# An FNet mixing layer and a gated feed-forward block on one core: a fifth unit of the sequence DFT as seven block products, and a planner that orders the DFTs' work

## The chip, the cores and the metric

The kernel runs on one core of a Trainium2 chip. The metric is device time in microseconds from launch to end, the median of three runs. Lower is better. The names of the engines in the profile are PE (TensorE, matrix products; PEld is its weight load), DVE (VectorE), ACT (ScalarE), POOL (GpSimd) and SP (SyncE, which here issues all DMAs).

## The reference

Two sublayers, each with a layernorm before it and a residual sum behind it, on 2048 tokens of 448 features, all in float32:

```python
def _A_ref(x, dft_seq_re, dft_seq_im, dft_hid_re, dft_hid_im):
    a = jnp.einsum("bsd,ed->bse", x, dft_hid_re)
    b = jnp.einsum("bsd,ed->bse", x, dft_hid_im)
    y = jnp.einsum("ts,bse->bte", dft_seq_re, a) - jnp.einsum("ts,bse->bte", dft_seq_im, b)
    return y

def _B_ref(x, w_gate, w_up, w_down):
    g = jnp.einsum("bsd,df->bsf", x, w_gate)
    u = jnp.einsum("bsd,df->bsf", x, w_up)
    h = _gelu(g) * u
    return jnp.einsum("bsf,fd->bsd", h, w_down)

x = A_x
h = x + _A_ref(_layernorm(x, axis=-1), A_dft_seq_re, A_dft_seq_im, A_dft_hid_re, A_dft_hid_im)
h2 = h + _B_ref(_layernorm(h, axis=-1), B_w_gate, B_w_up, B_w_down)
```

The feed-forward width is 1792. The DFT matrices are inputs, so the kernel multiplies by them as by any matrix.

## The kernel before

**Numbers.** Each float32 operand is split in two float16 parts: ACT writes the high part (`hi_part`, a scaled copy, line 105), DVE writes the low part as source minus high part (`lo_part`, lines 109 and 111). A product then takes three matmuls: high by high, high by low, low by high. So every operand of PE costs ACT and DVE one pass each, and DVE waits for ACT in it.

**Feature DFT (F).** The 16 tiles of 128 tokens are normalized (`x_stats`, `x_root`, `x_rstd`, `x_norm`, `x_lo`), transposed by DMA (`x_turn`; the first four by PE), and multiplied with both hidden matrices by `feature_mm` (line 422), 22 matmuls of 448 columns each, into two PSUM banks `ab`. `feature_out` takes the banks out: into `b`.

**Sequence DFT (U).** It has 8 passes `p`, each for 256 output tokens, and in each pass 8 units `u` of 256 input tokens (two tiles, `cc`). Unit (p, u) needs a block `wr` of both sequence matrices, 128 x 1024 in float32, loaded by `seq_load`, split into `ws` by `seq_split`, and multiplied with the `b` of its two tiles by `seq_mm` (line 518). A *plain* unit does this with 24 matmuls of 448 columns. A *product* unit (`is_s(u)`) uses a scheme of seven products for a 2 by 2 block product: 42 matmuls of 224 columns. For that DVE makes four sums of the block first (`seq_sums`, lines 480 to 482, into `wsum`), the split has seven slots and not four, and on the `b` side GpSimd makes sums of the tile's four halves (`feature_sums`, lines 460 to 462, on `b32`), which `feature_split` then splits. Units 4 to 7 are product units, 0 to 3 plain. `seq_out` takes a pass out of PSUM into `h`, and ACT and DVE then prepare the layernorm of the block that follows (`ffn_moments`, `ffn_norm_act`, `ffn_sums`, `ffn_split`, `ffn_transpose`).

**Weights of the gate and up products.** There are 14 rows `f` of weights. Ten of them are summed and split during the DFTs (`Weights`, `gu_raw` to `gu_w`) and stored in DRAM as `w_dram[f]`, whole; the last three in the order (2, 0, 1) also stay in SBUF as the first weights used. Four (`LATE`: 4, 7, 10, 13) are prepared later. Nine of the ten rows' tiles `gu_w`, and the `b32` of the product tiles, take turns in one ring of two buffers, tag `w`.

**What sets the order.** Each engine does its instructions in the order in which the program issues them, and SP its DMAs too. In the DFTs PE's work is a list of 80 slots (16 F, 64 U). All other work is hung on slots by hand: `plan(n, rank, what)` puts work ahead of slot `n`, for instance

```python
for g, (p, u) in enumerate(units):
    n = where["U", p, u]
    if is_s(u):
        plan(n - 3, 6, lambda p=p, u=u: seq_sums(p, u))
    if g:
        plan(n - 2, 3, lambda p=p, u=u: seq_split(p, u))
```

**After the DFTs.** A loop over 56 tiles `t` (four quarters of the tokens by 14 rows; line 970) does the gate and up products of `GateUp`: its PSUM banks X, Y and Z are opened, copied (`pY`, `u`) and closed in turn, ACT does the copies and the gelu. In the first quarter (t = 0 to 13) the weights of the down product are prepared beside that by `down_prep`: GpSimd sums (`down_sums`, `wd_s`), ACT high parts (`down_hi`), DVE low parts. From t = 14 on the down product (line 913) runs too.

Of the kernel before, what the change touches and what calls it, by code (L numbers as in the profile page):

```python
# [32 lines left out]
def kernel(  # L33
# [262 lines left out]
    S_UNITS, WR = (4, 5, 6, 7), 3  # L296
    ORDER = (0, 1, 5, 2, 6, 3, 7, 4)
# [141 lines left out]
    def feature_out(i):  # L439
        ps = feat.pop(i)  # L440
        if not is_s(i // 2):
            t = bop[i] = dft.tile([P, 2, 4, HD], F16, name=f"b{i}")
            for r in range(2):
                src, sc = ps[r][:, :D], (SC_AB, -SC_AB)[r]
                hi_part(t[:, 0, 2 * r : 2 * r + 2].rearrange("p o d -> p (o d)"), src, sc)
                lo_part(
                    t[:, 1, 2 * r : 2 * r + 2].rearrange("p o d -> p (o d)"),
                    src,
                    t[:, 0, 2 * r : 2 * r + 2].rearrange("p o d -> p (o d)"),
                    sc,  # L450
                )
            return
        b = b32[i] = ring.tile([P, 8, HD], F32, tag="w", bufs=2, name=f"b32_{i}")
        for r in range(2):
            hi_part(b[:, 2 * r : 2 * r + 2].rearrange("p o d -> p (o d)"), ps[r][:, :D], (SC_AB, -SC_AB)[r])


# [6 lines left out]
    def feature_split(i):  # L464
        b = b32.pop(i)
        t = bop[i] = dft.tile([P, 2, 7, HD], F16, name=f"b{i}")
        hi_part(t[:, 0], b[:, 1:8])
        lo_part(t[:, 1], b[:, 1:8], t[:, 0])
# [4 lines left out]
    def seq_load(p, u):  # L473
        wr[p, u] = dft.tile([P, 4, 2 * P], F32, tag="wr", bufs=4, name=f"wr{p}_{u}")
        nc.sync.dma_start(wr[p, u], w_seq[p * N_UNIT + u])

    def seq_sums(p, u):
        r = wr[p, u]
        s = wsum[p, u] = dft.tile([P, 4, 2 * P], F32, tag="wsum", bufs=2, name=f"wsum{p}_{u}")
        V.tensor_add(s[:, 0:2], r[:, 1:2].to_broadcast([P, 2, 2 * P]), r[:, 0:4:3])  # L480
        V.tensor_add(s[:, 2], s[:, 1], r[:, 0])
        V.tensor_add(s[:, 3], s[:, 2], r[:, 2])  # L482

    def seq_split(p, u):
        r = wr.pop((p, u))
        t = ws[p, u] = dft.tile([P, 2, 7, 2 * P], F16, tag="ws", bufs=3, name=f"ws{p}_{u}")
        parts = [(slice(0, 1), r[:, 0:1]), (slice(1, 3), r[:, 2:4]), (slice(3, 7), wsum.pop((p, u)))] if is_s(u) else [(slice(0, 4), r)]
        for dst, src in parts:
            hi_part(t[:, 0, dst], src, D_SC)
        for dst, src in parts:  # L490
            lo_part(t[:, 1, dst], src, t[:, 0, dst], D_SC)

# [15 lines left out]
    def seq_mm(p, u, first, last):  # L508
# [4 lines left out]
        for cc in range(2):  # L513
# [7 lines left out]
            if is_s(u):  # L521
                for a, o, k, half in PRODUCTS:
                    for m, (lb, lw) in enumerate(TERMS):
                        mm(k, slice(half * HD, half * HD + HD), w[:, lw, a, cc * P : (cc + 1) * P], b[:, lb, o], end and m == 2)
            else:
                for k, a0 in ((0, 0), (1, 1)):
                    for r in range(2):
                        for m, (lb, lw) in enumerate(TERMS):
                            rhs = b[:, lb, 2 * r : 2 * r + 2].rearrange("p o d -> p (o d)")
                            mm(k, slice(0, D), w[:, lw, a0 + 2 * r, cc * P : (cc + 1) * P], rhs, end and r == 1 and m == 2)  # L530
# [112 lines left out]
    for n, s in zip((2, 4, 6, 7), S_UNITS):  # L643
        mixed.insert(n, s)
# [12 lines left out]

    for k, (i, i2) in enumerate(tiles_of):
        n = where["F", i]
        if k >= 2:  # L660
            if k > 2:
                plan(n - 10, 8, lambda u=i // 2: x_load(u))
            if k > 2:
                plan(n - 7, 7, lambda i=i, j=i2: x_stats(i, j))
                plan(n - 6, 2, lambda i=i, j=i2: x_root(i, j))
                plan(n - 6, 5, lambda i=i, j=i2: x_rstd(i, j), lambda i=i, j=i2: x_bias(i, j))
            for c in (i, i2):
                n = where["F", c]
                if k > 2:
                    plan(n - 5, 5, lambda i=c: x_norm(i), lambda i=c: x_lo(i))  # L670
                plan(n - 4, 2, lambda i=c: x_turn(i))
        for c in (i, i2):
            n = where["F", c]
            if k:
                plan(n + 1, 1, lambda i=c: feature_out(i))
            if is_s(c // 2):
                plan(n + 1, 6, lambda i=c: feature_sums(i, G))
                plan(n + 2, 4, lambda i=c: feature_split(i))
    for g, (p, u) in enumerate(units):
        n = where["U", p, u]  # L680
        if is_s(u):
            plan(n - 3, 6, lambda p=p, u=u: seq_sums(p, u))
        if g:
            plan(n - 2, 3, lambda p=p, u=u: seq_split(p, u))
        if g < 4:
            if g:
                plan((-5, 1, 2)[g - 1], 9, lambda p=p, u=u: seq_load(p, u))
        else:
            plan(where["U", *units[g - 4]] - 2, 9, lambda p=p, u=u: seq_load(p, u))
# [3 lines left out]

    pairs = [where["F", 2 * u] for u in ORDER if is_s(u)]
    early_f = [s + 4 for s in pairs[1:3]]
    n0 = p1_end + 15
# [3 lines left out]
    order = list(reversed(in_dft[2:])) + in_dft[:2]  # L700

    def gu_begin(f):
        gu[f] = Weights(f, p2, lambda: w_tile(f"gu_w{f}", ring if f != 2 else ring3))

    late_f = N_DFT - len(early_f)
    at_f = early_f + [n0 + k * (len(slots) - 5 - n0) // late_f for k in range(late_f)]
    plan(0, 9, lambda: gu_begin(order[0]))
    for k, f in enumerate(order):
        n = at_f[k]
        plan(n, 7, lambda f=f: gu[f].sums())  # L710
        plan(n + 1, 7, lambda f=f: gu[f].split(True))
        if k + 1 < N_DFT:
            plan(n + 2, 9, lambda f=order[k + 1]: gu_begin(f))
        plan(n + 2, 7, lambda f=f: gu[f].split(False))
        plan(n + 3, 10, lambda f=f: gu[f].store())

    for p in range(N_PASS):
        q, j = divmod(p, 2)
        n = max(where["U", p, u] for u in range(N_UNIT)) + 1
        if p < 2:  # L720
            plan(n - 6, 9, lambda p=p: h_tile(p))
        else:
            n0 = min(where["U", p, u] for u in range(N_UNIT))
            plan(n0 - 5, 9, lambda p=p: h_tile(p))
            plan(n0 - 2, 4, lambda p=p: seq_seed(p))
        if p == N_PASS - 1:
            continue
        plan(n, 1, lambda p=p: seq_out(p))
        for g in range(2):
# [657 lines left out]
```

## Time and profile before

| | |
|---|---|
| median of 3 runs | 729.01 us (728.94 to 729.23) |
| the profiled execution | 729.15 us, of which the profile's span is 727.4 us |
| granted TensorE clock | 0.999 |
| busy share of the span | PE 97%, DVE 73%, ACT 54%, POOL 30% |
| DMA | 139.24 MB, 60.8% of 16 engines' span |
| first U slot to the end of the DFTs | 28.7 to 361.6 us |
| first quarter of gate and up | 361.6 to some 440 us |

How to read the lines that follow: a group's line has the source line, the engine, the operation, written and read tile with buffer numbers left out, the shape, the count, then busy time and mean ns of one, then the engine's idle time just before these instructions and what ended it. A timeline's line begins with start and length in us and ends with the idle time before it in brackets. A line of waits has who waited, for whom, the total, the number of times and the longest. Busy time of overlapping instructions of one engine is counted once.

### The profile page before, as it was taken

To read this page: it belongs to the slowest core of one execution; us is meant where nothing else is said; L and a number is where in the kernel's file an instruction comes from. 1 tells how busy PE (TensorE), PEld (TensorE's weight loads), DVE (VectorE), ACT (ScalarE), POOL (GpSimd) and SP (SyncE) were. 2 spreads that over 40 slices of the span, in tenths; PEclk is the share of its full clock that TensorE was granted. 3 is DMA by queue.
4 is the path that set the end of the run, shared out by engine and by line. 5 is a ranking of instruction groups with operands and counts; after the bars stand their busy time and mean duration, and the time that the engine had idled before them with its cause. 6 is when DMAs were issued, how large, how long until landed. Compare 5 with 4: busy or idle time off the path is not lost.

```text
span 727.4 us, 14930 instructions
## 1 busy us (share of the span) xinstructions
PE 708.2 (97%) x5944; PEld 574.1 (79%) x5944; DVE 529.1 (73%) x1054; ACT 396.1 (54%) x836; POOL 215.3 (30%) x241
## 2 busy tenths in 40 slices
PE   7999997989999999999998899999999999999998
PEld 5556555767777777686887789999999999999998
DVE  6777859698989998988478887576665756667520
ACT  5575646465757664645266665456555545555510
POOL 0023150000000000010025574465563756657230
PEclk9999999999999999999999999999999999999999
DMA  8464444656889697774268564957459486655401
GB/s 326 114 132 100 112 154 132 242 142 216 214 294 239 235 273 269 248 242 158 95 249 293 210 226 168 198 179 220 164 172 197 167 215 224 205 199 203 153 14 64
DMA packets 71765, 139.24 MB, mean 191 GB/s; under 512 B 41232, under 2 KB 47504, under 8 KB 71696
## 3 DMA queue, kind: packets, MB, share of 16 engines
q1 hardware_dynamic: 71696, 138.30, 60.8%
q8 instruction: 46, 0.75, 0.5%
q14 instruction: 23, 0.19, 0.1%
HBM read 108.79 MB, written 20.19 MB: 177 GB/s over the span
## 4 chain that ended last, share of the span: by engine, by line
PE 73%; DVE 13%; ACT 8%; issue 3%; DMA 2%; POOL 1%; SPq 0%; ACTq 0%; DVEq 0%
PE acc L518 29%; PE pY L970 13%; PE acc_d L913 11%; PE pX L970 8%; PE pZ L970 8%; DVE ws L111 2%; ACT ws L105 2%; ACT b L105 1%; DVE xs L109 1%; DVE st_x L328 1%; PE last_Z L1132 1%; PE last_X L1132 1%; PE last_Y L1132 1%; DVE b L109 1%; ACT x L355 1%
## 5 line engine op out<-in xcount | busy, mean ns | idle before, releaser
L518 PE MATMUL acc<-b,ws 128*128 128x224 f16 (+1 forms) x2112 | 277.4, 293 | 6.0 <-DVE ws L111 5.4
L518 PEld LDWEIGHTS <-ws 128*128 128x128 f16 x2112 | 202.8, 98 | 80.2 <-DVE ws L111 9.5
L970 PEld LDWEIGHTS <-gw 128*128 128x128 f16 x2067 | 201.9, 98 | 27.8 <-issue 7.3
L970 PE MATMUL pY<-hops,gw 128*128 128x256 f16 x901 | 122.5, 273 | 5.1 <-ACT pY L1009 5.1
L913 PE MATMUL acc_d<-wd,dn_w 128*128 128x224 f16 x882 | 105.1, 259 | 0.0
L111 DVE SCALAR_TENSOR_TENSOR ws<-wr,ws 128x256 f16<-128x256 f32 (+2 forms) x96 | 73.4, 790 | 19.3 <-ACT ws L105 18.7
L913 PEld LDWEIGHTS <-dn_w 128*128 128x128 f16 x882 | 85.0, 98 | 2.8
L105 ACT ACTIVATE ws<-wr 128x256 f16<-128x256 f32 (+2 forms) x96 | 63.0, 690 | 39.9 <-PE acc L518 21.5
L970 PE MATMUL pZ<-hops,gw 128*128 128x256 f16 x583 | 81.0, 273 | 0.8 <-DVE hh L980 0.7
L970 PE MATMUL pX<-hops,gw 128*128 128x256 f16 x583 | 79.2, 273 | 0.0
L1049 POOL TENSOR_TENSOR hh<-hh,c 128x256 f32<-128x256 f32 x42 | 32.1, 764 | 146.1 <-ACT c L1047 146.1
L215 POOL TENSOR_TENSOR wd_s<-wd 128x448 f32<-128x448 f32 x7 | 8.8, 1254 | 215.9 <-DVE wsum L480 199.3
L422 PEld LDWEIGHTS <-xT 128*128 128x128 f16 x352 | 34.2, 98 | 32.3 <-issue 1.2
L109 DVE TENSOR_TENSOR dn_w<-hh,dn_w 128x256 f16<-128x256 f32 x42 | 19.6, 467 | 53.1 <-ACT dn_w L105 53.1
L1063 POOL TENSOR_TENSOR dn_s<-hh 128x256 f32<-128x256 f32 x42 | 52.8, 1258 | 0.0
L105 ACT ACTIVATE ws<-wsum 128x1024 f16<-128x1024 f32 x32 | 33.6, 1050 | 35.1 <-DVE wsum L482 35.0
L109 DVE TENSOR_TENSOR dn_w<-dn_s,dn_w 128x640 f16<-128x640 f32 x42 | 46.3, 1103 | 6.2 <-ACT dn_w L105 4.4
L1014 ACT ACTIVATE u<-pY 128x256 f32<-128x256 f32 x56 | 21.5, 383 | 52.2 <-PE pY L970 52.1
L1009 ACT ACTIVATE pY<-pX 128x256 f32<-128x256 f32 x56 | 20.7, 369 | 49.1 <-PE pX L970 49.1
L422 PE MATMUL ab<-wh_hi,xT 128*128 128x448 f16 x224 | 45.5, 352 | 0.3 <-DVE b L111 0.2
L111 DVE SCALAR_TENSOR_TENSOR ws<-wsum,ws 128x1024 f16<-128x1024 f32 x32 | 39.1, 1222 | 2.6 <-ACT ws L105 2.6
L1062 POOL TENSOR_TENSOR dn_s<-hh 128x256 f32<-128x256 f32 x42 | 38.5, 916 | 0.0
(137 smaller groups left out, 937.0 us busy)
## 6 DMA issues: line engine op xcount, KB each, us to landing
gw<-w_dram SPq DMA_DIRECT2D x49, 896.0 KB, 4.8
wr<-in_w_seq_dram SPq DMA_DIRECT2D x64, 512.0 KB, 4.4
gu_raw<-in_w_gu_dram SPq DMA_DIRECT2D x28, 384.0 KB, 4.9
w_dram<-gu_w SPq DMA_DIRECT2D x10, 896.0 KB, 6.8
wd<-in_w_down_dram SPq DMA_DIRECT2D x14, 448.0 KB, 4.9
hx<-in_x_dram SPq DMA_DIRECT2D x8, 448.0 KB, 6.6
h_dram<-hx SPq DMA_DIRECT2D x8, 448.0 KB, 5.7
w_dram<-gw SPq DMA_DIRECT2D x4, 896.0 KB, 5.9
```

Source lines behind the costliest of these rows:

```text
L105: A.activation(dst, src, AF.Copy, scale=scale)
L109: V.tensor_sub(dst, src, hi)
L111: V.scalar_tensor_tensor(dst, src, scale, hi, op0=ALU.mult, op1=ALU.subtract)
L422: PE.matmul(feat[i][r][:, :D], xT[i][:, kx, :], w[:, kw, r * D : (r + 1) * D], start=n == 0, stop=n == 10,)
L518: PE.matmul(banks[k][:, cols], lhs, rhs, start=k not in begun, stop=stop, skip_group_check=True)
L913: PE.matmul(acc[k // 2][:, k % 2 * HD : (k % 2 + 1) * HD], a_of(la, a), b_of(lb, b), start=first and m == 0 and k % 2 == 0, stop=last and ...
L970: PE.matmul(ps, w[:, wl, wa + ws, :], ops[:, m + ms, :], start=first and n == 0, stop=last and n == len(terms) - 1, skip_group_check=True,)
L1014: A.activation(self.u2, self.Y, AF.Copy, scale=SC)
L1049: G.tensor_mul(c22, c22, self.c12)
L1062: G.tensor_add(s[:, 0:2], t[:, 0:2], t[:, 2:4])
L1063: G.tensor_sub(s[:, 2:4], t[:, 1:4:2], t[:, 0:4:2])
L1132: PE.matmul(banks[0][:, c * HD : (c + 1) * HD] if one else banks[c][:, 0:HD], last["h"][:, lh, f, tok], w, start=f == 0 and m == 0 and c = ...
```

## The change

1. **Unit 3 becomes a product unit**: `S_UNITS` is (3, 4, 5, 6, 7); plain are 0, 1 and 2. The order of the units in the first pass is now 0, 1, 5, 3, 6, 2, 7, 4, in the later passes 0, 3, 4, 1, 5, 2, 6, 7.
2. **Buffers**: `wr` has three and not four; `wsum` one and not two. The seven slots of a split are two tiles, `ws` (four slots, three buffers) and `wss` (the four sums, two buffers), written by four functions (`seq_high`, `seq_low`, `seq_high_s`, `seq_low_s`) where `seq_split` was one. `feature_out` and `feature_split` are each cut in a high and a low part, and `seq_copy` is cut from `seq_out`.
3. **A planner** (`Task`, `arranged`) in the kernel's Python takes the place of the slot numbers. Every piece of work has an engine, a length, a due time, the pieces it comes after, and a lag for those behind it (DMAs 5 to 7 us). Walking a clock of its own, it gives each engine that is free the ready piece with the earliest due time; the program then issues the work in the order of the starts found. PE's slots keep their order.
4. **Weight rows in pieces**: a row goes through four pieces, each split into a `stage` tile (two buffers) and stored by a DMA of its own. Nothing stays in SBUF; rows 0, 1 and 2, too, are loaded before they are used. The rows' work is spread evenly from the planner's time 50 on.
5. **In the first quarter**, ACT's high part of the sums `wd_s` (`down_hi(n, 1)`) is moved from the end of an odd tile to the middle of the next, behind `late_prep`.

```diff
-    S_UNITS, WR = (4, 5, 6, 7), 3
-    ORDER = (0, 1, 5, 2, 6, 3, 7, 4)
+    S_UNITS, WR_BUFS, WS_BUFS, WSS_BUFS, STAGE_BUFS = (3, 4, 5, 6, 7), 3, 3, 2, 2
+    ORDER = (0, 1, 5, 3, 6, 2, 7, 4)
...
-        wr[p, u] = dft.tile([P, 4, 2 * P], F32, tag="wr", bufs=4, name=f"wr{p}_{u}")
+        wr[p, u] = dft.tile([P, 4, 2 * P], F32, tag="wr", bufs=WR_BUFS, name=f"wr{p}_{u}")
...
+    def seq_high(p, u):
+        ws[p, u] = [dft.tile([P, 2, 4, 2 * P], F16, tag="ws", bufs=WS_BUFS, name=f"ws{p}_{u}")]
+        for t, dst, src in seq_parts(p, u):
             hi_part(t[:, 0, dst], src, D_SC)
...
+    def seq_high_s(p, u):
+        t = dft.tile([P, 2, 4, 2 * P], F16, tag="wss", bufs=WSS_BUFS, name=f"wss{p}_{u}")
+        ws[p, u].append(t)
+        hi_part(t[:, 0], wsum[p, u], D_SC)
...
+        def high(self, k):
+            self.stage[k] = p2.tile([P, 2, 4, P], F16, tag="stage", bufs=STAGE_BUFS, name=f"gu_p{self.f}_{k}")
+            src, t = self.piece(k)
+            hi_part(t[0], src, W_SC)
+
+        def low(self, k):
+            src, t = self.piece(k)
+            lo_part(t[1], src, t[0], W_SC)
+            s0, s1, _ = (self.parts(True) + self.parts(False))[k]
+            rows = w_dram[self.f].rearrange("p (l o d) -> p l o d", l=2, o=14)
+            nc.sync.dma_start(rows[:, :, s0:s1], self.stage[k][:, :, 0 : s1 - s0])
...
+    FIRST = 3
+    COST = {"F": 4.16, "P": 4.54, "S": 4.02}
...
+        load = add("SP", 0.1, T[n] - 12.0, lambda p=p, u=u: seq_load(p, u), after=done_with[g - WR_BUFS], lag=5.5)
...
+        high = add("A", size, T[n] - 1.6, lambda p=p, u=u: seq_high(p, u), after=[load] + room)
+        low = add("V", 1.14 * size, T[n] - 0.4, lambda p=p, u=u: seq_low(p, u), after=[high])
...
+            t = add("V", 1.35, T[n] - 2.8, lambda p=p, u=u: seq_sums(p, u), after=[load] + sums_of)
...
-    order = list(reversed(in_dft[2:])) + in_dft[:2]
+    order = in_dft
...
+        gap = (at_end - 10.0 - begin0) / N_DFT
+        t0 = begin0 + gap * k
...
+            stages.append(add("N", 0.0, 0.0, lambda: None, after=[low], lag=7.0))
...
+            for engine in ("SP", "N", "V", "A", "G"):
+                if busy[engine] > now:
+                    continue
+                able = [t for t in left if t.engine == engine and ready(t)]
+                if able:
+                    t = min(able, key=lambda t: t.due)
+                    cost = t.cost * (1.6 if engine == "V" and busy["G"] > now else 1.0)
+                    t.end = busy[engine] = now + cost
+                    begun.append((now, t))
...
+    gw_load(2)
     gw_load(3)
+    seq_copy(N_PASS - 1)
     seq_out(N_PASS - 1)
...
-            if n < NC - 1:
-                down_hi(n, 1)
...
             late_prep(2 * t)
+            if t > 0 and t % 2 == 0 and t < 2 * NC:
+                down_hi(t // 2 - 1, 1)
             nxt.z_open()
```

Three places in the order of the instructions. *ACT around the feature copies of tiles 14 and 15 (first pass).* `gu_w12`, `gu_p0`: a weight row and a piece of one; `b32`: the copy of a product tile. Before:

```order
L105 ACTIVATE gu_w12_992<-gu_raw12_422 128x512
L105 ACTIVATE gu_w12_992<-gu_raw12_422 128x256
L105 ACTIVATE ws0_6_1022<-wr0_6_449 128x256
L105 ACTIVATE ws0_6_1022<-wr0_6_449 128x512
L105 ACTIVATE ws0_6_1022<-wsum0_6_988 128x1024
L105 ACTIVATE gu_w12_992<-gu_s12_948 128x512 x2
L105 ACTIVATE b32_14_1062<-ab14_0_1038 128x448
L105 ACTIVATE b32_14_1062<-ab14_1_1039 128x448
L105 ACTIVATE b32_15_1093<-ab15_0_1069 128x448
```

Now:

```order
L105 ACTIVATE wss0_6_1080<-wsum0_6_1050 128x1024
L105 ACTIVATE gu_p0_0_1084<-gu_raw0_422 128x512
L105 ACTIVATE ws1_0_1087<-wr1_0_1038 128x1024
L105 ACTIVATE gu_p0_1_1089<-gu_raw0_422 128x256
L105 ACTIVATE b32_14_1119<-ab14_0_1054 128x448
L105 ACTIVATE b32_14_1119<-ab14_1_1055 128x448
L105 ACTIVATE b32_15_1178<-ab15_0_1095 128x448
```

The row has become pieces in tiles of their own, so `b32_15` no longer takes the buffer that `gu_w12` held, and splits for later units stand between the pieces.

*SP's queue after the first pass.* `gu_p`: the store of a piece; `wr`: the load of a unit's block. Before:

```order
L475 DMA wr1_4_1196<-in_w_seq_dram 128x1024
L475 DMA wr1_2_1247<-in_w_seq_dram 128x1024
L475 DMA wr1_5_1291<-in_w_seq_dram 128x1024
L575 DMA gu_raw9_1293<-in_w_gu_dram 128x768 x2
L475 DMA wr1_3_1331<-in_w_seq_dram 128x1024
L626 DMA w_dram11_162<-gu_w11_1242 128x3584
L475 DMA wr1_6_1383<-in_w_seq_dram 128x1024
```

Now:

```order
L637 DMA w_dram0_151<-gu_p0_3_1219 256x1x512
L475 DMA wr1_4_1269<-in_w_seq_dram 128x1024
L637 DMA w_dram1_152<-gu_p1_0_1311 256x1x512
L475 DMA wr1_1_1403<-in_w_seq_dram 128x1024
L637 DMA w_dram1_152<-gu_p1_1_1341 256x1x256
L593 DMA gu_raw2_1456<-in_w_gu_dram 128x768 x2
L637 DMA w_dram1_152<-gu_p1_2_1463 256x1x512
L475 DMA wr1_5_1468<-in_w_seq_dram 128x1024
```

Where one store stood among several loads, a store now stands between nearly every two.

*ACT in the first quarter, tiles 3 to 5.* `wd` from `wd_s`: the high part of the down weights' sums; `pY`, `u2`, `u3`, `g1`, `c12`: the copies and gelus of the tiles; `gw7`: a late weight row. Before:

```order
L1028 ACTIVATE u3_3_4482<-pY_3_4406 128x256
L1014 ACTIVATE u2_4_4501<-pY_4_4472 128x256
L105 ACTIVATE wd_4235<-wd32_1_4223 128x448
L105 ACTIVATE wd_4235<-wd_s_1_4452 128x1120
L105 ACTIVATE gw7_4521<-gu_raw7_4387 128x512
L1023 ACTIVATE g1_4_4530<-pX_4_4465 128x256
L1009 ACTIVATE pY_5_4539<-pX_5_4532 128x256
L1047 ACTIVATE c12_3_4514<-c12_3_4514 128x256
L1028 ACTIVATE u3_4_4549<-pY_4_4472 128x256
```

Now:

```order
L1159 ACTIVATE u2_4_4823<-pY_4_4794 128x256
L105 ACTIVATE wd_4557<-wd32_1_4545 128x448
L105 ACTIVATE gw7_4842<-gu_raw7_4708 128x512
L1168 ACTIVATE g1_4_4851<-pX_4_4787 128x256
L1154 ACTIVATE pY_5_4860<-pX_5_4853 128x256
L1192 ACTIVATE c12_3_4836<-c12_3_4836 128x256
L1173 ACTIVATE u3_4_4870<-pY_4_4794 128x256
L105 ACTIVATE gw7_4842<-gu_raw7_4708 128x256
L105 ACTIVATE wd_4557<-wd_s_1_4774 128x1120
L1159 ACTIVATE u2_5_4889<-pY_5_4860 128x256
```

The high part of the sums has moved six instructions back, behind `pY_5` and `u3_4`.

More of the change, by code (lines that the diff above doesn't have):

```diff
@@ L656, in plan, with __init__ @@
         at(todo, n, *((rank, w) for w in what))
+    class Task:
+        def __init__(self, engine, cost, due, what, after=(), begin=0.0, lag=0.1):
+            self.engine, self.cost, self.due, self.what = engine, cost, due, what
+            self.after, self.begin, self.lag = [t for t in after if t], begin, lag
+            self.end = None
+    FIRST = 3
+    COST = {"F": 4.16, "P": 4.54, "S": 4.02}
+    spans = [COST["F" if s[0] == "F" else "S" if is_s(s[2]) else "P"] for s in slots]
+    T = {n: sum(spans[FIRST:n]) - sum(spans[n:FIRST]) for n in range(len(slots) + 1)}
@@ new lines, with add, fixed @@
+    tasks, steps = [], {}
+    def add(*args, **kw):
+        tasks.append(Task(*args, **kw))
+        return tasks[-1]
+    for n in range(FIRST, len(slots)):
+        steps[n] = Task("PE", spans[n], T[n], None)
+    def fixed(n, rank, engine, cost, what, after=(), lag=0.0):
+        if n < FIRST:
+            plan(n, rank, what)
+            return None
+        return add(engine, cost, T[n + 1], what, after=after, begin=T[n] - 1.0, lag=lag)
+    turned, out_of, bop_of, ring_w = {}, {}, {}, []
@@ L708 @@
+    raw, freed, stages = None, [], []
     for k, f in enumerate(order):
[L709 to L739 removed]
@@ L800 @@
     x_root(a, b)
-    feature_out(0)
+    feature_high(0)
+    feature_low(0)
     x_rstd(a, b)
```

272 lines of the change are left out of this document (178 added, 94 removed).

## The prediction

> **What bounds the kernel now.** I read the shares of the span first, then the busy time stage by stage, then what TensorE waited for, and last the groups by shape for the prices.
>
> ```profile
> span 727.4 us, 14930 instructions
> PE   708.2 (97%) x5944; PEld 574.1 (79%) x5944; DVE 529.1 (73%) x1054; ACT 396.1 (54%) x836; POOL 215.3 (30%) x241
> ```
>
> TensorE (PE) is busy for 97% of the span, so whatever is gained must take matmul time away or take away one of its few waits. The stages show where those are (columns: stretch, its length, then busy time and instructions of PE, weight loads, DVE, ACT, POOL, the granted clock, and DMA):
>
> ```profile
> 28.70:88.50 59.80, 59.60 (x336) 32.60 (x335) 48.59 (x112) 37.52 (x65) 12.28 (x13) 1.00 0.56 125
> 88.50:100.80 12.30, 12.30 (x87) 8.32 (x86) 3.62 (x3) 3.76 (x5) 6.65 (x6) 1.00 0.44 165
> 100.80:156.00 55.20, 49.20 (x375) 34.81 (x373) 48.19 (x80) 32.66 (x56) 7.24 (x6) 1.00 0.51 170
> 156.00:293.00 137.00, 137.00 (x1058) 101.81 (x1056) 125.50 (x249) 85.91 (x163) 0.00 (x0) 1.00 0.81 247
> 293.00:361.60 68.60, 68.60 (x532) 51.07 (x530) 51.17 (x90) 33.59 (x65) 3.48 (x3) 1.00 0.56 188
> 361.60:440.60 79.00, 73.23 (x666) 64.80 (x664) 62.03 (x108) 50.87 (x120) 40.70 (x41) 1.00 0.66 240
> ```
>
> PE waits in two places: 6.0 us between 100.8 and 156 (the end of the first DFT pass and the second pass), and 5.8 us in the first quarter of the gate and up products (361.6 to 440.6). From 156 to 361.6 it never waits, while DVE is busy for 92% of 156 to 293 and 75% of the rest. The waits by name:
>
> ```profile
> PE acc L518 <- DVE ws L111: 5.4, 7, 1.3
> PE pY L970 <- ACT pY L1009: 5.1, 5, 1.2
> ACT b L105 <- DMA w_dram<-gu_w: 7.5, 1, 7.5
> ACT wd L105 <- POOL wd_s L218: 9.0, 5, 2.0
> ```
>
> So in the DFTs PE waits for DVE's splits of `ws`; behind that stands one long ACT wait, for the store of a weight row out of the `w` ring that the feature copies also use. In the first quarter five ACT waits of up to 2.0 us for GpSimd's `wd_s` sums become five PE waits.
>
> **TensorE time of the DFTs.** These rows give the pace:
>
> ```profile
> 28.71 4.70 PE L518 MATMUL acc<-b,ws 128*128 128x448 f16 x24
> 33.25 0.92 PE L422 MATMUL ab<-wh_hi,xT 128*128 128x448 f16 x4
> 360.81 0.93 PE L518 MATMUL acc<-b,ws 128*128 128x224 f16 x8
> 361.58 0.82 PE L970 MATMUL pX<-hops,gu_w 128*128 128x256 f16 x6
> L518 PE MATMUL acc<-b,ws 128*128 128x448 f16 x768 | 149.6, 352 | 0.1
> L518 PE MATMUL acc<-b,ws 128*128 128x224 f16 x1344 | 134.8, 259 | 5.9 <-DVE ws L111 5.4 <-DVE b L109 0.2
> ```
>
> The 24 wide matmuls of a plain unit take 33.25 - 28.71 = 4.54 us, 0.189 each; the narrow ones (361.58 - 360.81) / 8 = 0.096 each, so a product unit of 42 takes 4.02. The eight instances of unit 3 therefore save 8 x 0.52 = **4.2 us**. The stretch from 28.71 to 361.58 is 332.9 us long; 768 wide, 1344 narrow and 264 wide feature matmuls (12 tiles of 22) at these paces are 324 us. So about **9 us** in it are PE waits (more than the idle column shows, since a matmul counts as busy until it has drained). What the new order leaves of the 9 us I call S.
>
> **What DVE must do for it.** Rows for the price:
>
> ```profile
> 59.03 1.02 DVE L111 SCALAR_TENSOR_TENSOR ws<-wr,ws 128x256 f16<-128x256 f32 x2
> 154.64 2.36 DVE L111 SCALAR_TENSOR_TENSOR ws<-wr,ws 128x1024 f16<-128x1024 f32 x2
> L480 DVE TENSOR_TENSOR wsum<-wr 128x512 f32<-128x512 f32 x32 | 22.4, 701 | 0.0
> L482 DVE TENSOR_TENSOR wsum<-wsum,wr 128x256 f32<-128x256 f32 x32 | 15.3, 478 | 1.1
> L481 DVE TENSOR_TENSOR wsum<-wsum,wr 128x256 f32<-128x256 f32 x32 | 13.9, 436 | 1.1
> 57.99 1.12 DVE L111 SCALAR_TENSOR_TENSOR b<-ab,b 128x448 f16<-128x448 f32 x2
> 97.64 2.17 DVE L109 TENSOR_TENSOR b<-b,b 128x1568 f16<-128x1568 f32 x1 [8.69 <-ACT b L105]
> 99.73 1.68 DVE L111 SCALAR_TENSOR_TENSOR ws<-wr,ws 128x1024 f16<-128x1024 f32 x1
> 101.90 1.79 DVE L109 TENSOR_TENSOR b<-b,b 128x1568 f16<-128x1568 f32 x1 [0.49 <-ACT b L105]
> L460 POOL TENSOR_TENSOR b<-b 128x448 f32<-128x448 f32 x8 | 11.2, 1396 | 80.7 <-ACT b L105 63.2 <-DVE ws L111 17.5
> 156.00:293.00 137.00, 18.43 (x36) 6.79 (x12) 1.00 0.81 247
> ```
>
> A product unit needs one split of 1024 columns, as a plain unit does (1.14 back to back), and besides that the split of three slots (0.95 without the overlap) and the sums (0.70 + 0.44 + 0.48): 2.55 us of DVE more, 20.4 for eight. Two feature tiles change from 1.12 to 1.79: 1.4 more. GpSimd gets sums for two more tiles; its L460 alone takes 1.40 each, and I take 3.3 with the two smaller ones, 6.6 in all. While GpSimd ran, DVE's split at 97.64 took 2.17 against 1.79 and the one at 99.73 1.68 against 1.2. Those lose some 0.4 us each, about a third of the GpSimd time beside them: 2.4 us more for DVE.
>
> [...]
>
> Now stage by stage. *28.7 to 156:* DVE was busy 48.6 + 3.6 + 48.2 = 100.4 us and idle 26.9. It gets two units (5.1), the tiles (1.4), GpSimd's part (2.4) and about 0.6 weight rows more (the planner starts rows at its time 50 and every 26.4 us; a row costs about 4: the last line above counts 18.4 us of DVE for the sums and half the splits of six rows in 156 to 293, and the other half of the splits is some 0.9 each): 2.4. That is 111.7 us. PE's own time there would be 127.3 - 9 - 1.0 = 117.3, so DVE may idle for 5.6 us before PE waits. Of its 26.9 idle us, 8.7 stand in front of one instruction at 97.64, behind the ring's store, and go: weight rows leave the ring for two stage buffers. Of the other 18 I let a little over half remain under an order that fills gaps with whatever is ready, 9.6: S gets **4**. The ends: all 18 remain (12.5), or under 5.6 (0).
> *156 to 293:* DVE 125.5, plus four units (10.2), less 0.9 weight rows (3.6): 132.1 us, in 134.9 of PE time. It may idle 2.8 us. It idled 11.5 before, mostly because it was ahead of its buffers; I take 4.8, S gets **2** (ends 0 and 8.7).
> *293 to 361.6:* 51.2 + 5.1 in 67.6: nothing. ACT's extra copies of an added unit are fewer than DVE's instructions, and ACT has 51 us free in 156 to 293, so they cost nothing as long as they stand behind no wait.
> So S = 6, between 0 and 21. The cover for all of this is DVE's lead over PE, some two units of 4 us by the three `ws` buffers; where it is gone each late split is a PE wait.
>
> **DMAs and the smaller edits.** Forty stores of pieces take the place of ten whole rows on SP's queue, and each may hold up the `wr` load behind it. Three `wr` buffers for four: a load is freed by the last split three units back, 12.6 us before its need; landing takes 4.4, sums and splits some 4, which leaves 4. I cost both at nothing, between 0 and 1 us for a dozen loads each.
>
> ```profile
> wr<-in_w_seq_dram SPq DMA_DIRECT2D x64, 512.0 KB, 4.4
> gw<-w_dram SPq DMA_DIRECT2D x49, 896.0 KB, 4.8
> w_dram<-gu_w SPq DMA_DIRECT2D x10, 896.0 KB, 6.8
> ```
>
> Rows 0 to 2 of the weights are now loaded again before the gate and up products. 0 and 1 start five slots ahead (20 us against 4.8); row 2 waits for its buffer until the pools close, and is read by the third tile, some 6.5 us after 361.6: 0 to 1 us, I take **0.3**. ACT's six splits of the sums move behind `u3` half a tile later.
>
> ```profile
> 381.39 0.97 POOL L218 TENSOR_TENSOR wd_s<-wd 128x224 f32<-128x224 f32 x1
> 382.40 1.14 ACT L105 ACTIVATE wd<-wd_s 128x1120 f16<-128x1120 f32 x1 [1.68 <-POOL wd_s L218]
> 383.44 0.61 ACT L105 ACTIVATE gw<-gu_raw 128x512 f16<-128x512 f32 x1
> 384.23 0.37 ACT L1009 ACTIVATE pY<-pX 128x256 f32<-128x256 f32 x1
> 384.65 1.36 PE L970 MATMUL pY<-hops,gw 128*128 128x256 f16 x11 [1.22 <-ACT pY L1009]
> 384.83 0.37 ACT L1028 ACTIVATE u<-pY 128x256 f32<-128x256 f32 x1
> ```
>
> The sums ended at 382.36 and the new place is after 384.83, so the wait goes. Behind the split in its new place stands only the copy `u2`, whose readers come after the next tile's eleven `pX` matmuls. I take the whole 5.1 us; the ends are 5.8 (all idle of the stage) and -1.7 (each of six splits of 1.14 in PE's way instead).
>
> **The sum.** 729.15 (profiled execution; span 727.4 and 1.75 around it) - 4.2 - 9.0 + S - 5.1 + 0.3 = 711.15 + S. The median of the runs is 0.14 lower: 711.0 + S. With S = 6: **717.0 us**.
>
> **Rivals.** *The order hides everything* (S at most 3: 711 to 714): speaks for it that a piece of a weight row has no due time near and fills any gap; against it, 98% of DVE in the middle passes. *DVE becomes the bound* (S 9 to 16.5: 720 to 727.5): its idle stays, since much of it was waiting for ACT's high parts, which a queue in order cannot fill; for it 48.2 of 55.2 us before, in a stage where PE stood still for DVE. *Slower than before:* the stage buffers couple the queues. ACT's high part of a piece waits for the store of the piece two before; that store waits on SP behind a `wr` load that waits for DVE; and the next `ws` high part stands behind it on ACT. One such wait cost 7.5 us of ACT above. With 40 pieces it decides where they cost PE 0.45 us each on the mean: S = 18, no gain; at 0.55 each (S = 22) 733 us. Speaks against it that the planner gives a store 7 us, and a whole row took 6.8.
>
> **Chances.** Forecast (S 3 to 9) 0.42, everything hidden 0.22, DVE the bound 0.20; S 16.5 to 19.5, no difference, 0.06; slower 0.10. Differences within 0.2% (1.5 us) can't be told from none. Range: from S = 0 with the first quarter at its best (710.5) to where the third case ends (727): it leaves out the last two cases. Faster 0.84, same 0.06, slower 0.10.
>
> **What would show it.** Right: PE's wait for `pY` near 0 and ACT's for `wd_s` gone; L518 with 576 wide and 1680 narrow matmuls; DVE over 95% busy in the middle passes; no ACT wait for a `w_dram` store over 2 us. Wrong: PE waits for `ws` well above 6 us after 156 (the budget of the middle passes), or ACT waits for stage stores, or a wait in front of the third gate tile.

## The result, and the profile after

The changed kernel takes 721.0 us (median of 4 runs, 719.75 to 721.3) against 729.1 us beside it: a ratio of 0.9886, with a 95% interval of 0.9869 to 0.9903. The forecast was 717.0 us. The profiled execution took 721.3 us, of which the span is 719.5. The page's first lines and the clock of its 40 slices:

```profile
span 719.5 us, 15439 instructions
PE 704.9 (98%) x6088; PEld 590.3 (82%) x6088; DVE 553.0 (77%) x1092; ACT 406.0 (56%) x854; POOL 222.5 (31%) x247
PEclk9999899999999999999999999999999999999999
```

DVE has 24 us more to do than before, PE 3 us less, and one slice of the clock reads 8, which none did before the change. By stages, with the columns of the prediction's table:

```profile
28.80:75.00 46.20, 46.20 (x267) 25.83 (x265) 42.08 (x86) 34.52 (x57) 20.91 (x18) 1.00 0.57 136
75.00:90.00 15.00, 11.77 (x69) 8.12 (x68) 14.79 (x30) 6.95 (x12) 0.00 (x0) 0.77 0.25 56
90.00:120.00 30.00, 30.00 (x206) 19.72 (x204) 25.23 (x31) 17.11 (x27) 13.33 (x12) 1.00 0.44 157
120.00:168.00 48.00, 45.66 (x403) 38.27 (x401) 46.07 (x96) 30.94 (x62) 0.00 (x0) 1.00 0.77 239
168.00:293.00 125.00, 125.00 (x1036) 99.68 (x1035) 117.72 (x234) 80.25 (x151) 0.00 (x0) 1.00 0.79 239
293.00:358.00 65.00, 65.00 (x553) 53.06 (x551) 52.27 (x96) 33.33 (x64) 3.50 (x3) 1.00 0.68 234
358.00:437.00 79.00, 76.94 (x705) 68.64 (x704) 67.95 (x115) 53.10 (x125) 42.83 (x44) 1.00 0.71 251
```

What PE lost stands in two lines: 75 to 90, where it was idle for 3.2 us and had a mean clock of 0.77, and 120 to 168. From 168 to 358 it never waits, though DVE is 94% busy to 293. The DFTs' stretch, from the first U slot to the end of the last, is 28.83 to 357.91, 329.1 us in place of 332.9: 3.8 won. What follows the DFTs won 4.2, and the start lost 0.1. The waits that matter:

```profile
PE acc L533 <- DVE wss L111: 5.6, 3, 3.2
PE pZ L1115 <- DVE hh L1125: 1.9, 3, 1.0
ACT ws L105 <- DMA wr<-in_w_seq_dram: 11.9, 8, 3.3
DVE wsum L480 <- DMA wr<-in_w_seq_dram: 7.3, 5, 2.4
```

All three waits of the DFTs are now for the low part of `wss`, the split of a product unit's sums. PE's wait for `pY`, ACT's for `wd_s` and ACT's 7.5 us for a weight row's store are gone, and no ACT wait for a stage store took their place. The matmuls of the DFT units (576 wide ones, 720 + 960 narrow ones):

```profile
L533 PE MATMUL acc<-b,wss 128*128 128x224 f16 x960 | 120.5, 262 | 5.6 <-DVE wss L111 5.6
L533 PE MATMUL acc<-b,ws 128*128 128x448 f16 x576 | 112.7, 352 | 0.0
L533 PE MATMUL acc<-b,ws 128*128 128x224 f16 x720 | 96.5, 261 | 0.0
```

The large wait is at U(0,3), the first appearance of the new product unit. Timelines of ACT, POOL, DVE and PE (start, length, ..., the idle time before):

```profile
59.79 1.04 ACT L105 ACTIVATE wss<-wsum 128x1024 f16<-128x1024 f32 x1
...
70.55 1.90 DVE L109 TENSOR_TENSOR b<-b,b 128x1568 f16<-128x1568 f32 x1 [0.61 <-ACT b L105]
70.89 2.08 POOL L461 TENSOR_TENSOR b<-b 128x224 f32<-128x224 f32 x1
...
74.55 1.79 DVE L109 TENSOR_TENSOR b<-b,b 128x1568 f16<-128x1568 f32 x1 [2.09 <-ACT b L105]
...
77.11 1.15 DVE L111 SCALAR_TENSOR_TENSOR b<-ab,b 128x448 f16<-128x448 f32 x2
78.18 1.22 DVE L111 SCALAR_TENSOR_TENSOR wss<-wsum,wss 128x1024 f16<-128x1024 f32 x1
...
79.45 0.37 PE L533 MATMUL acc<-b,wss 128*128 128x224 f16 x1 [3.23 <-DVE wss L111]
```

ACT had the high part of this `wss` ready at 60.83. Its low part could have run from then on, but the planner had put it on DVE behind the low parts of tiles 6 and 7, which this unit needs too, behind those of tiles 12 and 13, which only a later unit needs (the ones at 70.55 and 74.55; the second waited 2.09 us for ACT, which waited for GpSimd's 2.08 us sum), behind six small operations and behind tile 4's low part. PE stood from 76.2 to 79.45. What it then lost besides, the clock of single microseconds shows (the number before the last two):

```profile
77.00:78.00 1.00, 0.00 (x0) 0.00 (x0) 0.96 (x3) 0.76 (x1) 0.00 (x0) 1.00 0.00 0
78.00:79.00 1.00, 0.00 (x0) 0.00 (x0) 1.00 (x2) 0.98 (x3) 0.00 (x0) 0.70 0.00 0
...
84.00:85.00 1.00, 1.00 (x7) 0.82 (x6) 1.00 (x4) 0.71 (x1) 0.00 (x0) 0.50 0.06 9
85.00:86.00 1.00, 1.00 (x9) 0.74 (x7) 1.00 (x3) 1.00 (x3) 0.00 (x0) 0.89 0.05 6
```

The granted clock was 0.50 from about 78.4 to 85.2, which is 6.8 us, of which PE worked through 5.8 at half speed. U(0,3) took 10.2 us in place of 4.02: 3.4 of wait and 2.8 of slow work. The other two waits are 0.7 us at U(1,4) and 2.1 us at U(2,4).

### The profile page after: what moved, and what is told of

Its sections match the earlier page's. It is cut to its first block, busy times and chain, and to the rows that moved or that the text cites. A ratio compares the mean times of both kernels' runs of the same rounds, so it can differ in the third digit from the quotient of the medians.

```text
span 719.5 us, 15439 instructions
## 1 busy us (share of the span) xinstructions
PE 704.9 (98%) x6088; PEld 590.3 (82%) x6088; DVE 553.0 (77%) x1092; ACT 406.0 (56%) x854; POOL 222.5 (31%) x247
## 4 chain that ended last, share of the span: by engine, by line
PE 73%; DVE 17%; DMA 2%; ACT 2%; issue 2%; POOL 1%; SPq 0%; DVEq 0%; ACTq 0%; POOLq 0%
PE acc L533 28%; PE pY L1115 12%; PE acc_d L1060 11%; PE pZ L1115 8%; PE pX L1115 8%; DVE ws L111 2%; PE ab L422 2%; DVE xs L109 1%; DVE wss L111 1%; DVE b L109 1%; PE last_Z L1277 1%; PE last_X L1277 1%; PE last_Y L1277 1%; DVE wd L111 1%; DMA wr<-in_w_seq_dram 1%
## 5 line engine op out<-in xcount | busy, mean ns | idle before, releaser
L1115 PEld LDWEIGHTS <-gw 128*128 128x128 f16 x2184 | 213.4, 98 | 25.1 <-issue 3.2
L533 PE MATMUL acc<-b,ws 128*128 128x224 f16 (+1 forms) x1296 | 205.8, 302 | 0.0
L533 PEld LDWEIGHTS <-ws 128*128 128x128 f16 x1296 | 126.3, 98 | 54.0 <-DVE ws L111 0.3
L1115 PE MATMUL pY<-hops,gw 128*128 128x256 f16 x952 | 129.1, 273 | 0.0
L533 PE MATMUL acc<-b,wss 128*128 128x224 f16 x960 | 120.5, 262 | 5.6 <-DVE wss L111 5.6
L533 PEld LDWEIGHTS <-wss 128*128 128x128 f16 x960 | 93.3, 99 | 7.1 <-DVE wss L111 6.3
L1115 PE MATMUL pZ<-hops,gw 128*128 128x256 f16 x616 | 85.6, 273 | 2.2 <-DVE hh L1125 1.9
L105 ACT ACTIVATE wss<-wsum 128x1024 f16<-128x1024 f32 x40 | 42.1, 1052 | 41.5 <-DVE wsum L482 32.7
L422 PEld LDWEIGHTS <-xT 128*128 128x128 f16 x352 | 34.2, 98 | 32.4 <-issue 1.5
L1208 POOL TENSOR_TENSOR dn_s<-hh 128x256 f32<-128x256 f32 x42 | 52.2, 1243 | 0.0
L111 DVE SCALAR_TENSOR_TENSOR wss<-wsum,wss 128x1024 f16<-128x1024 f32 x40 | 49.8, 1244 | 1.4 <-ACT wss L105 1.4
```

The costliest lines, as they stand in the source:

```text
L105: A.activation(dst, src, AF.Copy, scale=scale)
L111: V.scalar_tensor_tensor(dst, src, scale, hi, op0=ALU.mult, op1=ALU.subtract)
L422: PE.matmul(feat[i][r][:, :D], xT[i][:, kx, :], w[:, kw, r * D : (r + 1) * D], start=n == 0, stop=n == 10,)
L533: PE.matmul(banks[k][:, cols], lhs, rhs, start=k not in begun, stop=stop, skip_group_check=True)
L1115: PE.matmul(ps, w[:, wl, wa + ws, :], ops[:, m + ms, :], start=first and n == 0, stop=last and n == len(terms) - 1, skip_group_check=True,)
L1208: G.tensor_sub(s[:, 2:4], t[:, 1:4:2], t[:, 0:4:2])
```

## The experiments

Each is compared with the kernel before on the same chip (729.2 to 729.4 us). "Waits" below are the gaps between PE's matmuls beyond their pace in the DFTs.

**One DVE instruction, moved to where its input is ready.** In the list that the planner returns, `wss0_3`'s low part goes ahead of the low part of tile 13:

```
+    begun = [t for _, t in arranged()]
+    begun.remove(marks["wss", 0, 3])
+    begun.insert(begun.index(marks["b", 13]), marks["wss", 0, 3])
```

> Changed kernel; on DVE alone, the low part of wss0_3 stands ahead of b13's low part instead of behind b12, b13, r_x8 and b4. Theory (one instruction placed badly, and the clock that falls while PE stands still): the 3.4 us wait at U(0,3) and the 2.8 us of slow clock behind it both go, the granted clock is 0.999, and the kernel takes about 715 us (721 less 6). Rival (DVE is the bound of 28.8 to 168, its work only moved): the sums of b12, b13 and b4 that now come later make PE wait at U(1,4), U(2,4) or in front of the next units, and 719 to 721 us remain.

Measured: 718.89 us (718.71 to 718.97; ratio 0.9856, 0.9843 to 0.987). The wait at U(0,3) and its slow clock are gone (PE is busy for all of 75 to 90), but 1.3 us of waits come at U(0,4), 0.8 at U(1,3), and at U(1,4) a wait of 2.8 with a slow clock of its own behind it. Of 6.2 us that the move took away, 4.1 came back on balance by U(2,4): the rival was nearer. DVE's and PE's timelines at U(1,4) say what stands there:

```profile
121.34 0.43 DVE L482 TENSOR_TENSOR wsum<-wsum,wr 128x256 f32<-128x256 f32 x1
121.69 1.15 DVE L570 SCALAR_TENSOR_TENSOR hx<-acc,hx 128x448 f32<-128x448 f32 x2
...
124.20 1.15 DVE L578 TENSOR_TENSOR hx<-hx,e 128x448 f32<-128x448 f32 x2
125.27 1.22 DVE L111 SCALAR_TENSOR_TENSOR wss<-wsum,wss 128x1024 f16<-128x1024 f32 x1
...
126.54 0.27 PE L533 MATMUL acc<-b,wss 128*128 128x224 f16 x1 [2.64 <-DVE wss L111]
```

The mix of pass 0's result (L570 to L578, 3.6 us) falls between the sums of the fourth product unit in a row and their split.

**The same instruction, one place earlier only**: the last line with `marks["b", 4]`.

> Changed kernel; the same low part of wss0_3 only one place earlier on DVE, ahead of b4's low part (two instructions, 1.07 us). Theory of the clock: the wait falls from 3.4 to about 2.3 us, too short for the clock to drop, and the gain is 1.1 + 2.8 = 3.9 us: about 717 us, clock 0.999. Rival (the slow stretch has nothing to do with the length of the wait): the gain is the 1.1 us alone: about 720 us, clock still near 0.995.

Measured: 718.68 us (717.89 to 719.19; ratio 0.9853, 0.9839 to 0.9866). The wait was 2.3 us as planned, but the clock fell all the same:

```profile
79.00:80.00 1.00, 0.91 (x9) 0.90 (x10) 1.00 (x3) 1.00 (x3) 0.00 (x0) 0.93 0.00 0
80.00:81.00 1.00, 1.00 (x7) 0.80 (x6) 1.00 (x4) 0.97 (x3) 0.00 (x0) 0.50 0.00 0
...
83.00:84.00 1.00, 1.00 (x11) 0.93 (x10) 1.00 (x2) 0.00 (x0) 0.00 (x0) 0.87 0.36 74
```

It was slow for 3.4 us, half as long as in the changed kernel, and U(0,3) took 1.7 us more for it. That 2.3 us of idle time is too short for the clock to drop was wrong; the gain of 2.3 us lies between what the two theories gave.

**PE kept busy through the wait.** 48 matmuls of 64 columns into the free columns of a bank, in front of the matmul that waits; nothing reads their result:

```
+                        if (p, u, cc, a, m) == (0, 3, 0, 6, 2):
+                            for _ in range(48):
+                                PE.matmul(banks[0][:, D:512], w[0][:, 0, 0, 0:P], b[:, 0, 0, 0:64], start=False, stop=False, ...)
```

> Changed kernel with 48 matmuls of 64 columns, whose results nothing reads (free columns of a PSUM bank), put on PE in front of the matmul of U(0,3) that waits. DVE and ACT do as before, so the wait ends at the same time. Theory of the clock: PE is busy for most of the wait, the clock stays at full speed, and the time falls by the 2.8 us of slow work to about 718 us, though PE does more. Rival (slow for another reason): 721 us, the slow stretch from 78 to 85 us is still there.

Measured: 719.24 us (718.51 to 720.01; ratio 0.9865, 0.985 to 0.988). They filled 1.5 of the 3.4 us; the wait ended when it did before, and the clock stayed up:

```profile
75.00:90.00 15.00, 13.18 (x132) 9.40 (x131) 14.65 (x30) 7.16 (x13) 2.29 (x1) 1.00 0.29 63
```

The four executions list a mean clock of 0.998 to 1.000, where those of the changed kernel list 0.995 to 0.997. So the slow stretch comes from PE's standing idle, and 2.8 us of U(0,3) were its price: PE work that nobody needs made this unit that much shorter (7.4 us in place of 10.2). The DFTs' stretch got 2.4 us shorter, 326.6 us; the other 0.4 came back as waits, since PE now came sooner to the units where DVE is late (1.8 us at U(1,4), 1.0 at U(2,4), 0.5 at U(5,4), 3.2 in all in place of 2.8). The medians differ by 1.8 us, but the four executions spread over 1.5.

**The moved down sums alone**, in the kernel before:

```
-            if n < NC - 1:
-                down_hi(n, 1)
...
+            if t > 0 and t % 2 == 0 and t < 2 * NC:
+                down_hi(t // 2 - 1, 1)
```

> The kernel before with one edit of the change alone: ACT's high parts of the down sums stand behind the second half's copies instead of in the next tile. Theory: this gives the 4.2 us that the changed kernel won behind the DFTs (forecast: 4.8), so about 724.7 us. Rival (those 4 us came from other things that changed with it, such as the weight rows loaded again or DVE's state at the end of the DFTs): 727 us or more.

Measured: 725.61 us (724.87 to 726.24; ratio 0.9949, 0.9936 to 0.9961), 3.5 us less; the profiled execution's span is 4.3 less. The gaps of the first quarter fall from 7.1 to 2.7 us, as in the changed kernel (3.0). This one edit is nearly half of the change's gain.

**Unit 3 plain again**, the rest as changed (`S_UNITS = (4, 5, 6, 7)`, `ORDER = (0, 1, 5, 2, 6, 3, 7, 4)`, insertions at 2, 4, 6, 7):

> Changed kernel with the planner, the pieces and the moved down sums, but unit 3 plain again (and its old place in the order). TensorE work is 4.2 us more, DVE work some 20 us less. Theory (DVE's extra work for the fifth product unit makes the PE waits, 6 to 9 us in the changed kernel and its variants so far): the waits fall to 0 to 2 us, and it takes 716 to 718 us, no longer than the changed kernel, so the product unit itself earned nothing. Rival (the waits come from the planner's order and GpSimd, and stay): 723 us or more, and the product unit is worth its 4.2 us.

Measured: 720.06 us (718.76 to 722.66; ratio 0.9868, 0.9853 to 0.9883). That is not longer than the changed kernel, so in the change as it stands the fifth product unit earned nothing that can be measured. But the waits did not fall to 0 to 2 us: 5.5 remain, with 24 us less on DVE. Neither theory had this; DVE's waits for `wr` loads, 19.5 us in seven of them between 120 and 293, pointed elsewhere (below).

**The tiles' sums on DVE** (`add("V", 1.1, ..., feature_sums(i, V))` for `add("G", 3.4, ..., feature_sums(i, G))`):

> Changed kernel with the sums of the ten product feature tiles on DVE instead of GpSimd (three tensor operations a tile, some 1.1 us by the widths). DVE gets 11 us of work and loses the 11.5 us that its instructions lost beside GpSimd; ACT's copy behind the sums starts 2 us a tile sooner. Theory (a late chain ACT, GpSimd, ACT, DVE puts wss0_3 behind): the wait at U(0,3) and the slow clock go, 1 to 4 us of waits are left in the second and third pass: 714 to 717 us. Rival (DVE is full in the stretch whoever does the sums): 718.5 to 721 us, the waits only move to U(1,4) and U(2,4).

Measured: 719.51 us (718.49 to 720.29; ratio 0.9866, 0.9852 to 0.9879): the rival. In the profiled execution (720.29 us, mean granted clock 0.995) the wait at U(0,3) is 0.7 us, and U(1,4) has 3.1 us of wait and 2.9 of slow work. The other three executions (718.49 to 719.55 us) list a clock of 1.000, so that slow work does not come in every execution. Groups of DVE from 28 to 125, of the changed kernel and then of this one, give the price of GpSimd beside DVE:

```profile
L480 DVE TENSOR_TENSOR wsum<-wr 128x512 f32<-128x512 f32 x7 | 5.9, 847 | 2.4 <-DMA wr<-in_w_seq_dram 2.4
L481 DVE TENSOR_TENSOR wsum<-wsum,wr 128x256 f32<-128x256 f32 x7 | 4.8, 688 | 0.2
L482 DVE TENSOR_TENSOR wsum<-wsum,wr 128x256 f32<-128x256 f32 x7 | 4.5, 639 | 0.2
```

```profile
L459 DVE TENSOR_TENSOR b<-b 128x448 f32<-128x448 f32 x10 | 6.2, 617 | 0.0
L480 DVE TENSOR_TENSOR wsum<-wr 128x512 f32<-128x512 f32 x7 | 4.8, 680 | 0.0
L460 DVE TENSOR_TENSOR b<-b 128x224 f32<-128x224 f32 x10 | 3.9, 392 | 0.3
L461 DVE TENSOR_TENSOR b<-b 128x224 f32<-128x224 f32 x10 | 3.9, 391 | 0.3
L481 DVE TENSOR_TENSOR wsum<-wsum,wr 128x256 f32<-128x256 f32 x7 | 3.0, 425 | 0.2
L482 DVE TENSOR_TENSOR wsum<-wsum,wr 128x256 f32<-128x256 f32 x7 | 3.0, 425 | 0.2
```

Seven units' sums took 15.2 us beside GpSimd and 10.8 without; the ten tiles' sums cost DVE 14.0 us (11 expected). Moving them is nearly even for DVE (555.5 us busy in place of 553.0); it shortens the chain through ACT: DVE's idle time in front of the ten tiles' splits, for ACT's high parts, fell from 4.8 to 2.6 us.

**Weight rows later** (that kernel with `begin0 = 110.0`):

> As the last (sums on DVE), and the planner starts the second weight row at its time 110 instead of 50: some two rows, 4 us of DVE each, move from the first two passes to the middle and last ones, where DVE has 7 and 13 us free. Theory (DVE is short locally, in the first two passes): 1 to 3 us less than with the sums on DVE alone, about 713 us. Rival (DVE is short on the whole): the waits move to the passes after 168 us and the time is the same within 1 us.

Measured: 725.44 us (724.78 to 726.45; ratio 0.995, 0.9938 to 0.9962), 6 us worse, a miss for both. PE waits 0.7 and 0.9 us up to U(1,4), 9.2 us from 156 to 293 and 1.3 at 336; ACT's waits for `wr` loads rise to 20.9 us. All rows now had to go into less time, at 25.8 us of DVE in 168 to 293 in place of 20.1 (21.7 in the changed kernel), with due times that put them ahead of splits. Between 215 and 225 SP also held two `wr` loads behind four transposes and a store; how much that added was not separated.

**A plain unit between the product units** (the kernel with the sums on DVE, pass 1 in the order 0, 1, 3, 4, 2, 5, 6, 7):

> The kernel with the sums on DVE, and one edit to it: in the second pass the plain unit 1 stands ahead of units 3 and 4 (order 0, 1, 3, 4, 2, 5, 6, 7 in place of 0, 3, 4, 1, 5, 2, 6, 7), so that the four product units (0,7), (0,4), (1,3), (1,4) no longer follow each other. The work is the same. Theory (DVE is short locally, in those four): the 3.1 us wait at U(1,4) and the slow clock behind it go, and 714 to 716 us remain. Rival (DVE's shortage is the sum of all work up to there): the wait only moves by a unit or a pass, 718 to 720 us.

Measured: 718.37 us (717.49 to 719.01; ratio 0.9846, 0.9832 to 0.986): the rival. The wait at U(1,4) fell from 3.1 to 0.5 us and the clock is 1.00 throughout the DFTs, but 6.5 us of small waits, none over 1.9, are spread from 76 to 195.

**Row pieces due 30 us later**, besides. The planner's price of a product unit's sums also goes from 1.35 to 1.55 us; in this kernel the two were not tried apart:

```
+            t = add("V", 1.55, T[n] - 2.8, lambda p=p, u=u: seq_sums(p, u), ...)
...
+        due = lambda part: t0 + gap * part + 30
```

> As the last, and the pieces of the weight rows are due 30 us later for the planner (they fill gaps instead of standing ahead of splits), its price of a product unit's sums 1.55 in place of 1.35 us. Theory (row work that stood ahead of splits took DVE's lead): waits of 0 to 2 us are left in the DFTs, the clock stays at 1.00: 711.5 to 714 us, which the prediction's sum gives for S of 0 to 2. Rival (DVE is full on the whole from 28 to 168 us, so that later row work comes back in the middle passes): 716 to 719 us.

Measured: **714.15 us** (713.7 to 714.54; ratio 0.979, 0.9777 to 0.9803), the fastest of all and some 7 us under the changed kernel. Three gaps are left in the DFTs: 1.7 us at U(0,3), 0.2 and 0.1. DVE's row work in 125 to 168 fell from 7.7 to 4.0 us and came back in 168 to 293 (19.4 to 22.1) and from 293 to the end of the DFTs (8.8 to 10.6); though DVE is 95% busy in 168 to 293, PE does not wait there:

```profile
120.00:168.00 48.00, 48.00 (x417) 39.87 (x416) 46.52 (x101) 33.57 (x67) 0.00 (x0) 1.00 0.72 217
168.00:293.00 125.00, 125.00 (x1049) 100.69 (x1047) 119.21 (x234) 80.01 (x155) 0.00 (x0) 1.00 0.76 237
```

**Unit 3 plain in that kernel**, and then **with four `wr` buffers** (`WR_BUFS` 4 for 3, nothing else; the planner, which knows the number, arranges the work anew):

> As the last (sums on DVE, rows due later), but unit 3 plain and in its place of the kernel before. Theory: with DVE 20 us less loaded its waits are near 0, and it takes 4.2 us of TensorE work more than the last kernel less the waits that that one has left: 716 to 718 us. Then the product unit is worth 2 to 4 us once the order is right, against about 1 us lost in the order of the change. Rival (the product unit takes back its gain under any order): within 1 us of the last kernel.

> The last kernel with unit 3 plain, which took 724.5 us though DVE has 20 us less to do, with four buffers for wr instead of three (its smaller feature tiles leave the room). In the kernel with three, DVE stood 21.4 us in five waits for wr loads between 120 and 293, the longest 6.3. Theory (three buffers: a load can start only when DVE has done the split three units back, so a late DVE makes its own next load late): these waits fall below 6 us, PE's waits from 7 to 0 to 2 us: 717 to 719.5 us. Rival (the loads stand on SP behind transposes and stores of pieces, whatever the buffers): 722.5 us or more.

Measured: 724.48 us (722.88 to 726.83; ratio 0.9933, 0.9916 to 0.9949) with three, a miss for both theories, and 717.03 us (716.27 to 717.71; ratio 0.983, 0.9816 to 0.9844) with four, as its theory had it. DVE's waits for `wr` of the one and of the other:

```profile
DVE wsum L480 <- DMA wr<-in_w_seq_dram: 23.0, 6, 6.3
```

```profile
DVE wsum L480 <- DMA wr<-in_w_seq_dram: 0.5, 1, 0.5
```

With three buffers a load starts when DVE has done the split three units back (between 28 and 293 SP stood 22.8 us for such splits in front of nine `wr` loads); a late DVE thereby delays its own next input, and stands idle while PE runs dry (3.8 us of PE's time from 168 to 293, none with four). The fourth buffer, with the order that the planner makes for it, gives back 7.45 us. So the fair comparison is 717.03 us (plain, four buffers) with 714.15 (product, three): the product unit is worth 2.9 us of its 4.2 once the order is right. The product kernel with four buffers was not tried; no run shows whether its larger feature tiles leave room for one.

**Row pieces later, in the changed kernel with the one instruction moved:**

> The changed kernel with the low part of wss0_3 ahead on DVE, as in the first of these runs, and the pieces of the weight rows due 30 us later; sums on GpSimd, order of the units and all prices as in the change. Theory (row pieces that stand ahead of splits are what makes DVE late at U(0,4) to U(2,4)): of the 7 us of waits and slow clock that the first run had left, 0 to 3 remain: 712.5 to 715 us. Rival (GpSimd beside DVE, and the four product units in a row): 717 to 719 us, with a wait of over 2 us at U(1,4) still there.

Measured: 717.21 us (716.41 to 717.69; ratio 0.9834, 0.982 to 0.9848), 1.7 us less than without the later due times. The waits after 126 are gone, the one at U(1,4) is not:

```profile
PE acc L533 <- DVE wss L111: 3.5, 3, 3.0
```

The rival was right: there the mix of pass 0 stands in front of the split, as after the first move, at the end of four product units in a row. Of the combinations tried, only the one with the due times, the order of pass 1, the sums' place and the new price together leaves no more than 2 us of waits.

## Why the prediction came out as it did

- **TensorE work, -4.2:** as forecast, in the counts above and in units of 4.02 us.
- **Old waits, -9.0:** gone, with the row's store in front of ACT.
- **S, forecast 6:** this term was too small. The stretch won 3.8 us, so S was 13.2 - 3.8 = 9.4. For the middle passes 2 was right (2.1, all at U(2,4); after 168 none), though DVE was 94% busy there and not over 95%. For the first passes it was 6.9 instead of 4 (6.2 at U(0,3), 0.7 at U(1,4); the remaining 0.4 lies in gaps too small to name), and 2.8 of that is no wait: it is matmul time at a clock of 0.50 behind one. The sum had counted a wait at its own length. The fill of 48 matmuls shows that part by itself. The other part is DVE's lateness, and the first move shows it: of the 6.2 us that it took away at U(0,3), 4.1 came back at the next units.
- **GpSimd's share of S:** forecast 2.4 us more of DVE's time, from a third of GpSimd's time beside it. GpSimd was busy for 34.2 us in 28.8 to 120, and DVE's instructions of 40 to 75 and 90 to 120 took some 11.5 us longer there than their forms do elsewhere (about 7 before): some 4 more, and still a third. One stretch of this trace has both sides of it:

```profile
96.11 0.66 POOL L460 TENSOR_TENSOR b<-b 128x224 f32<-128x224 f32 x1
96.25 2.17 DVE L109 TENSOR_TENSOR b<-b,b 128x1568 f16<-128x1568 f32 x1 [1.67 <-ACT b L105]
...
96.85 2.09 POOL L461 TENSOR_TENSOR b<-b 128x224 f32<-128x224 f32 x1
```

DVE's split, 1.78 us elsewhere, began 0.52 us before GpSimd's sum ended and took 0.4 us longer. GpSimd's next sum, 0.66 us at its shortest, began during the split, ended 0.52 us after the split's end and took 2.09; the sum at 70.89 above, of 2.08, did the same (0.51). So the loss falls on both. The ten tiles would take GpSimd 24.5 us at the shortest of each sum (1.13, 0.66 and 0.66), so by this estimate GpSimd itself lost 9.7 of the 34.2 us; DVE's loss of 11.5 us is a third of them.

- **First quarter, -5.1 + 0.3:** 4.2 won. The waits for `pY` went; three waits of `pZ` for `hh`, 1.9 us in all, are what was late next: in front of the longest, which ended at 408.47, stand two of DVE's row sums of 0.95 us each, 0.42 at their shortest, while GpSimd works. There is no wait in front of the third gate tile. The 0.6 us missing here and the 3.4 us of S make up the 4.0 us by which the forecast was too low; no error hid another.
- **Three `wr` buffers, at nothing:** not safe. In the changed kernel DVE stood 7.3 us for `wr`; with unit 3 plain the fourth buffer and the order made for it decided 7.45 us. Its price in the changed kernel itself stays open.
- **Rivals:** 721.0 lies in the range given for "DVE becomes the bound" (720 to 727.5) and not in the likeliest case (714 to 720). DVE is the bound from 28 to 168 us, but of an order and not of its total work: a better order of nearly the same work has its stretch at 322.0 us, S = 2.3 and 714.15 us, where the sum 711.0 + S gives 713.3. Stage buffers did not couple the queues as the slower rival had it: in the changed kernel no ACT wait for a stage store is listed. The lower end of the range, 710.5, is 710.0 by the sum's own terms (S = 0, 5.8 for 5.1 and no 0.3); nothing here hangs on it.

## What to carry to other kernels

Price a wait of a busy TensorE by what follows it too: after single waits of 2.3 to 3.4 us the clock fell here to 0.50 for 3.4 or 6.8 us, and U(0,3) lost 2.8 us by that besides its wait of 3.4. Before an added product is judged, look at the busiest other engine stage by stage and at what stands in its queue in front of the one instruction that the product needs; with DVE above 90% (91% in 28.8 to 75, 99% in 75 to 90), moving one instruction moved most of the wait and its slow clock (4.1 of 6.2 us). A buffer fewer can take away the lead that lets that engine fill its idle time; with unit 3 plain it showed as waits for loads, 23.0 us with three `wr` buffers against 0.5 with four.

## What the hardware showed

Inside the DFTs the clock's slow stretches had two lengths only, by the granted clock, which read 0.50 in them: 3.4 us after idle times of 2.3, 2.8 and 3.1 us (the one-place move, the first move, the last run), 6.8 us after 3.4 and 3.1 us (the change, the sums on DVE). Shorter gaps in a row did it too: in the kernel with the moved sums alone, three of 1.5, 0.3 and 0.8 us within 3.2 us stand ahead of 3.4 slow ones, and in the kernel with later rows three of 2.0, 0.3 and 1.6 us within 4.2 us (a mean clock of 0.99 in 168 to 293). But the kernel before has the same three gaps of 1.5, 0.3 and 0.8 us at the same place (110.37 to 113.58 us), and its clock stays at 1.00. So the idle times alone do not decide, and 3.1 us were followed by 3.4 slow us in one run and by 6.8 in another. What else decides, no run shows. Single idle times up to 1.9 us cost nothing beyond themselves: with the plain unit between the product units, where the longest was 1.9, the clock was 1.00 throughout the DFTs. After a single wait the clock fell 2.2 to 4.3 us after PE stopped, in three of the five cases when PE already worked again.
